# Retention and a rational feed-forward layer on one core: the first four units in quarters, and new orders for steps 0 to 31

## The chip, the core and the metric

One core of a Trainium2 chip. Its engines run their own instruction streams in order and wait for each other by semaphores: PE (TensorE, matmuls into PSUM), DVE (VectorE), ACT (ScalarE), POOL (GpSimd), and SP, whose queue issues all DMAs here. The metric is the device time of one execution in microseconds (us).

## The reference

```python
def _attn_ref(q, k, v):                    # (8, 8, 576, 64): batch, heads, tokens, head size
    scores = (1/sqrt(64)) * q @ k.T
    gamma = 1 - 2.0 ** (-5 - arange(8))    # one per head
    rel = pos[:, None] - pos[None, :]
    Dmat = where(rel >= 0, gamma ** rel, 0)
    return (scores * Dmat) @ v

def _moe_ref(x, w_in, w_out, a, b):        # x: 4608 x 512, w_in: 512 x 2048, w_out: 2048 x 512
    h = x @ w_in
    P = a0 + a1*h + a2*h**2 + a3*h**3
    Q = 1 + |b0|*|h| + |b1|*h**2
    return (P / (Q + 1e-6)) @ w_out
```

`x` is the first function's output, heads side by side. Everything is float32, the weights arrive as float64 bits (read as int64).

## The kernel before, in words

**Retention.** The 4608 tokens are 36 units of 128, for all eight heads (four pairs). The decay matrix is split into factors: q is multiplied by powers of gamma that grow along the unit (`scale_q`), v by powers that fall (`scale_v`), so that only a triangular 0/1 mask is left between scores and output (`decay`), and what came ahead of a unit enters by a state `S` that is carried on (`add`) and faded (`fade`, on POOL). A unit of the later kind is done in quarters, two halves of 64 tokens on either side (`visit`): scores and state sums of unit k on 64x64 matmuls in four corners of the array, and beside them the output of the unit before (`put`, `of_inside`, `of_before`). Its state in the middle of a unit is made by DVE (`middle`). Rows of the array that write one bank are kept apart by a no-op on the SP queue that PE signals and then waits for (`follow`, L377).

Units 0 to 3 are done otherwise in this kernel (`whole_scores`, `whole_state`, `whole_decay`, `whole_outputs`, `whole_add`): 128 tokens at a time, with a 128x128 mask `whole_sb` and a PSUM tile `early` for the state sums. For units 0 to 3 the second layout of k is not loaded but made by four transposes on PE (`turn`) into the PSUM tile `unread`, and a copy by ACT (`keep_turned`, called kn in the orders). Unit n's raw inputs are the tiles qk n and kv n.

**Feed-forward.** Four units make a block of 512 tokens, nine blocks. x is split into a high part (`xhi`, ACT) and a low part (`xlo`, DVE). A step is one block b and one slice f of 128 of the 2048 inner columns: `gemm1` makes h (12 matmuls of 512 columns), then come p, u, v (p the polynomial, u = |h|, v the denominator): `ffn_p` (ACT and DVE), `ffn_p2` (DVE), `ffn_va` (v's linear step, on DVE or ACT by the table VA), `ffn_v` (DVE), `ffn_r` (ACT, Ln and Exp into u), `ffn_q`, `ffn_q3` (DVE), `ffn_hi` (ACT) and `ffn_lo` (the low part of g, on DVE or POOL by LO). `gemm2` of a step comes three or four steps later. Steps 0 to 7 are the first half of block 0, 8 to 23 block 1, 24 to 31 the other half of block 0, and from 32 on block by block. In steps 8 to 20 the tile u lies in PSUM (`free_at`).

**Weights.** Each of 32 weight tiles is loaded as bits and put together by ACT (two instructions, `c` and `bits`, or `held`), merged by DVE (`c<-c,bits`), copied as a high part by ACT (`w`) and its low part made by DVE or POOL (table WLO). All this goes on up to step 23 beside the steps.

**Order.** All four compute engines take instructions in the order in which the program issues them (`InOrder`). That order is written out: `BEFORE0` to `BEFORE4` for the stretch ahead of step 0 (the head), one list a unit; FIRST0 to FIRST23, MID (steps 8 to 20), DENSE and DENSE_ALONE (24 to 31) for the steps; REST from step 32 on. `run` (L650) goes through a list; words whose work there is none of are passed over. STARTS says how many weight tiles are begun in a step, LOADS in which order units and weights are loaded, SCALES and SCALES_Q which engine scales v and q of units 0 to 8.

Of the kernel before, what the change touches and what calls it, by code (L numbers as in the profile page):

```python
# [30 lines left out]
NP = 4  # L31

BEFORE0 = "warm_a outputs warm_b scores split3 turn keep_hi scale_v split1 start kn state split0 scale_q decay add fade split2 keep_lo decay1".split()
BEFORE1 = "turn outputs scale_q scores kn warm_b split0 start keep_hi state warm_a split1 decay add scale_v fade decay1 split3 split2 keep_lo".split()
BEFORE2 = "turn scores scale_v kn split3 split0 outputs warm_a state warm_b keep_hi decay split2 start decay1 scale_q split1 add keep_lo fade".split()
BEFORE3 = "split0 split1 warm_a turn outputs kn scores keep_hi split3 decay split2 state decay1 start keep_lo add scale_q scale_v fade warm_b".split()
BEFORE4 = "split3 outputs state keep_hi scores split0 start keep_lo decay scale_q split1 add scale_v fade split2".split()
FIRST0 = "scale_v split3 gemm1 split2 ffn_hi visit ffn_r scale_q split0 ffn_q decay ffn_p start keep_hi ffn_p2 keep_lo ffn_va ffn_v decay1 gemm2 ffn_lo add split1 ffn_q3 fade".split()
FIRST1 = "visit gemm1 keep_hi decay ffn_p split3 ffn_p2 scale_v ffn_r ffn_va decay1 add split2 fade ffn_q ffn_hi start split1 scale_q keep_lo ffn_v split0 ffn_q3 gemm2 ffn_lo".split()
FIRST2 = "gemm1 visit ffn_hi split1 decay scale_q ffn_p gemm2 split3 split2 keep_hi ffn_lo decay1 add ffn_va scale_v ffn_r ffn_v keep_lo fade start ffn_p2 split0 ffn_q ffn_q3".split()  # L40
# [6 lines left out]
FIRST22 = "visit scale_q split1 gemm1 split0 decay scale_v ffn_p split3 keep_hi decay1 ffn_hi ffn_p2 gemm2 ffn_r ffn_q add keep_lo fade start ffn_lo ffn_q3 split2 ffn_va ffn_v".split()
FIRST23 = "split0 gemm1 ffn_p split3 visit decay ffn_va ffn_v gemm2 ffn_hi scale_q ffn_p2 keep_hi keep_lo split2 decay1 ffn_r add ffn_lo fade ffn_q scale_v split1 ffn_q3 start".split()
MID = "start gemm1 split1 ffn_p ffn_hi ffn_r ffn_p2 gemm2 ffn_va ffn_lo split2 ffn_q ffn_v ffn_q3 split3 split0".split()
DENSE = "scale_q gemm1 visit decay ffn_p split0 ffn_hi split1 ffn_va ffn_r gemm2 ffn_lo keep_hi ffn_v ffn_p2 split2 split3 scale_v ffn_q ffn_q3 decay1 add keep_lo fade".split()  # L50
DENSE_ALONE = "gemm1 ffn_r ffn_p visit decay decay1 ffn_p2 ffn_q keep_hi split2 ffn_va add scale_v ffn_hi split3 ffn_v fade scale_q gemm2 split0 ffn_lo keep_lo ffn_q3 split1".split()
# [6 lines left out]
STARTS_BEFORE = "0 0 2 2 2".split()  # L58
LOADS = "unit | weight unit unit weight weight | weight unit weight weight unit weight | weight".split()
STARTS = "0 2 2 1 3 1 0 1 0 0 1 1 1 1 1 2 1 0 2 2 1 1 1 1".split()  # L60
# [28 lines left out]
def retention_ffn(ctx: ExitStack, tc: tile.TileContext, qkv, w_in, w_out, consts, masks, out):  # L89
# [49 lines left out]
    firsts = op.tile([P, 2, DM], F32, tag="o0", name="whole_sb")[:, 0, 0 : 2 * P]  # L139
    whole_sb, unit_sb = firsts[:, 0:P], firsts[:, P:]  # L140
# [6 lines left out]
    def warm(n, by=None):  # L147
        by = gq_sb[:, 0] if by is None else by
# [86 lines left out]
    def place_of(a, k):  # L235
        by_acc = k is not None and k <= NP and k != 2
# [3 lines left out]
    def places(a, k):  # L240


        apart = a is None or k is not None and k <= NP
# [59 lines left out]
    early = ps_h.tile([P, 2, NPAIR, D], F32, tag="h", name="early")  # L303

    def whole_scores(n):


        q, kt = (raws[n][0][:, i] for i in range(2))
        ps = sums[n] = place_of(None, n)
        for g in range(NPAIR):  # L310
            for j in range(2):
                r = slice(j * D, j * D + D)
                pe.matmul(ps[:, j, g * P : (g + 1) * P], kt[r, g], q[r, g], start=True, stop=True, skip_group_check=True)

# [6 lines left out]

    def whole_state(n):
        kn, v = (raws[n][1][:, i] for i in range(2))
        for g in range(NPAIR):
            for j in range(2):
                o = early[j * D : (j + 1) * D, n % 2, g, :]
                pe.matmul(o, kn[:, 2 * g + j, :], v[:, 2 * g + j, :], start=True, stop=True, skip_group_check=True)

    def whole_ret(n, j):
        return raws[n][0][:, 1] if j == 0 else raws[n][1][:, 0].rearrange("p (g x) d -> p g (x d)", g=NPAIR)  # L330

    def whole_decay(n, j):
        m = whole_sb.unsqueeze(1).broadcast_to([P, NPAIR, P])
        dve.tensor_tensor(whole_ret(n, j), sums[n][:, j].rearrange("p (g i) -> p g i", g=NPAIR), m, ALU.mult)

    def whole_outputs(n):
        q, v, o = raws[n][0][:, 0], raws[n][1][:, 1], sums_of(n)
        for j in range(2):
            ret = whole_ret(n, j)
            for c in range(2):  # L340
                for e in range(2):
                    pe.matmul(o[e * D : (e + 1) * D, j, c, :], v[:, 4 * c + 2 * e + j, :], ret[:, 2 * c + e, :], start=c == 0, stop=True, skip_group_check=True)
        if n % 9:
            for c in range(2):
                for j in range(2):
                    for e in range(2):
                        r = slice(j * D, j * D + D)
                        pe.matmul(o[e * D : (e + 1) * D, j, c, :], state[n][r, 2 * c + e, :], q[r, 2 * c + e, :], start=False, stop=True, skip_group_check=True)

# [333 lines left out]
    def load_more(n):  # L683


        for what in loading:
            if what == "|":
                return
# [91 lines left out]
```

## Time and profile before

| what | us |
|---|---|
| runs (3) | 873.03, 874.12, 875.38 |
| profiled execution | 873.48 |
| its span | 871.7 |
| PE busy | 851.0 (98%) |
| DVE busy | 774.6 (89%) |
| ACT busy | 664.8 (76%) |
| POOL busy | 131.5 (15%) |
| chain that ended last | PE 81%, DVE 11%, ACT 4% |

The span is that of the program's instructions; the execution's own time lies 1.8 us above it. Busy shares are means over stages that differ: in the first stretch PE works in pieces of less than a microsecond and waits between them, from step 32 on it runs without a break.

### The profile page before, as it was taken

To read this page: it belongs to the slowest core of one execution; us is meant where nothing else is said; L and a number is where in the kernel's file an instruction comes from. 1 tells how busy PE (TensorE), PEld (TensorE's weight loads), DVE (VectorE), ACT (ScalarE), POOL (GpSimd) and SP (SyncE) were. 2 spreads that over 40 slices of the span, in tenths; PEclk is the share of its full clock that TensorE was granted. 3 is DMA by queue.
4 is the path that set the end of the run, shared out by engine and by line. 5 is a ranking of instruction groups with operands and counts; after the bars stand their busy time and mean duration, and the time that the engine had idled before them with its cause. 6 is when DMAs were issued, how large, how long until landed. Compare 5 with 4: busy or idle time off the path is not lost.

```text
span 871.7 us, 18740 instructions
## 1 busy us (share of the span) xinstructions
PE 851.0 (98%) x7574; PEld 727.6 (83%) x7574; DVE 774.6 (89%) x1222; ACT 664.8 (76%) x1239; POOL 131.5 (15%) x107
## 2 busy tenths in 40 slices
PE   8899999999999999999999999999999999999996
PEld 7657787778888888888888888888888888888885
DVE  4999999999899888898889988898898899888994
ACT  3898999988767778777877787778777787667773
POOL 2532323621001110111111110000111111000000
PEclk9999999999999999999999999999999999999999
DMA  9895000033121112111211121111211121001001
GB/s 343 310 355 221 1 2 0 2 104 112 36 92 50 49 50 98 49 50 50 97 50 50 49 98 50 49 50 57 70 39 41 42 97 50 1 2 48 1 1 48
DMA packets 20806, 64.55 MB, mean 74 GB/s; under 512 B 2544, under 2 KB 2672, under 8 KB 20720
## 3 DMA queue, kind: packets, MB, share of 16 engines
q1 hardware_dynamic: 20720, 63.36, 20.8%
q8 instruction: 59, 0.97, 0.4%
q14 instruction: 27, 0.22, 0.1%
HBM read 53.91 MB, written 9.44 MB: 73 GB/s over the span
## 4 chain that ended last, share of the span: by engine, by line
PE 81%; DVE 11%; ACT 4%; issue 2%; DMA 1%; POOL 0%; SPq 0%; ACTq 0%; DVEq 0%; POOLq 0%
PE acc L85 37%; PE h L85 36%; DVE p L85 5%; PE ps L85 4%; DVE v L85 3%; PE y L85 2%; DVE c L85 1%; PE psNone L85 1%; ACT free_at L85 1%; ACT g L85 1%; DMA qk<-in_qkv 1%; DVE qk L85 0%; ACT bits L85 0%; ACT c L85 0%; ACT u L85 0%
## 5 line engine op out<-in xcount | busy, mean ns | idle before, releaser
L85 PE MATMUL h<-xhi,w 128*128 128x512 f32 x1152 | 367.8, 381 | 3.9 <-DVE p L85 3.2
L85 PE MATMUL acc<-w,g 128*128 128x512 f32 x1584 | 367.8, 381 | 3.4 <-ACT o L85 1.6
L85 PEld LDWEIGHTS acc<-w,g 128*128 128x128 f32 x1584 | 296.2, 189 | 49.4 <-ACT o L85 2.0
L85 PEld LDWEIGHTS h<-xhi,w 128*128 128x128 f32 x1152 | 217.7, 189 | 38.0 <-DVE p L85 3.1
L85 ACT ACTIVATE p<-h,const_sb 128x512 f32<-128x512 f32 x144 | 111.5, 774 | 164.1 <-PE h L85 157.5
L85 PE MATMUL h<-xlo,w 128*128 128x512 f32 x576 | 218.4, 379 | 0.1
L85 DVE TENSOR_TENSOR p<-p,h 128x512 f32<-128x512 f32 x144 | 98.5, 684 | 41.0 <-ACT u L85 38.6
L85 PEld LDWEIGHTS h<-xlo,w 128*128 128x128 f32 x576 | 108.9, 189 | 16.7 <-issue 1.1
L85 DVE SCALAR_TENSOR_TENSOR p<-p,const_sb,h 128x512 f32<-128x512 f32 x144 | 107.3, 745 | 4.0
L85 ACT ACTIVATE v<-u,absb 128x512 f32<-128x512 f32 x129 | 103.3, 801 | 0.3 <-DVE p L85 0.2
L85 DVE SCALAR_TENSOR_TENSOR p<-v,p 128x512 f32<-128x512 f32 x140 | 99.0, 707 | 3.3
L85 DVE TENSOR_TENSOR v<-v,u 128x512 f32<-128x512 f32 x131 | 101.4, 774 | 0.2 <-ACT v L85 0.2
L85 DVE SCALAR_TENSOR_TENSOR p<-p,const_sb,u 128x512 f32<-128x512 f32 x131 | 99.3, 758 | 1.2 <-ACT u L85 1.2
L85 POOL TENSOR_TENSOR S<-S,const_sb 128x256 f32<-128x256 f32 x32 | 27.1, 848 | 454.9 <-DVE S L85 454.9
L85 DVE SCALAR_TENSOR_TENSOR v<-v,u 128x512 f32<-128x512 f32 x131 | 89.4, 683 | 0.0
L85 ACT ACTIVATE u<-u 128x512 f32<-128x512 f32 x131 | 82.6, 630 | 4.1
L85 ACT ACTIVATE g<-p 128x512 fp32r<-128x512 f32 x132 | 82.7, 627 | 3.4 <-DVE p L85 3.1
L85 ACT ACTIVATE u<-v 128x512 f32<-128x512 f32 x131 | 82.0, 626 | 3.1 <-DVE v L85 3.1
L85 DVE TENSOR_TENSOR g<-p,g 128x512 fp32r<-128x512 f32 x115 | 78.6, 684 | 2.6 <-ACT g L85 2.6
L85 ACT ACTIVATE u<-h 128x512 f32<-128x512 f32 x131 | 76.7, 586 | 2.5 <-DVE v L85 2.4
L85 ACT ACTIVATE kv<-kv,const_sb 128x64 f32<-128x64 f32 x232 | 58.2, 334 | 4.6 <-DMA kv<-in_qkv 4.6
L85 POOL TENSOR_TENSOR qk<-qk,const_sb 128x512 f32<-128x512 f32 x31 | 48.7, 1573 | 39.0 <-DMA qk<-in_qkv 39.0
(93 smaller groups left out, 714.9 us busy)
## 6 DMA issues: line engine op xcount, KB each, us to landing
qk<-in_qkv SPq DMA_DIRECT2D x36, 512.0 KB, 4.1
kv<-in_qkv SPq DMA_DIRECT2D x32, 512.0 KB, 5.9
bits<-in_w_in SPq DMA_DIRECT2D x16, 512.0 KB, 8.8
bits<-in_w_out SPq DMA_DIRECT2D x16, 512.0 KB, 7.4
out<-o SPq DMA_DIRECT2D x28, 256.0 KB, 4.0
out<-o SPq DMA_DIRECT2D x16, 128.0 KB, 2.1
kv<-in_qkv SPq DMA_DIRECT2D x4, 256.0 KB, 6.7
const_sb<-in_consts SPq DMA_DIRECT2D x1, 265.0 KB, 2.9
```

Of the source, the lines that this page charges most:

```text
L85: return lambda *a, **k: self.tc.keep_in_program_order(method(*a, **k))
```

## The change

The four units of the head go through the same functions as later units: `visit(None, n)` for scores and state sums, `decay`, `add`, `fade`, then `put`. The five `whole_` functions, the tile `early` and the 128x128 mask are gone; `turn` and `keep_turned` stay. In place of five lists, the table LOADS and two counts there is one list HEAD with a word for each piece of work and each load, with the unit's number behind it (W is the load of a weight tile, begin starts putting one together, merge and halve carry it on). All lists for steps 0 to 31 but REST and END, and STARTS, SCALES, SCALES_Q, VA, LO and WLO are new.

```diff
-NP = 4
-
-BEFORE0 = "warm_a outputs warm_b scores split3 turn keep_hi scale_v split1 start kn state split0 scale_q decay add ...
...
+HEADED = 4
+
+HEAD = (
+    "U0 M scale_q0 turn0 U1 kn0 scale_v0 visit0 scale_q1 turn1 U2 kn1 turn2 decay0 scale_v1 add0 fade0 visit1"
+    " scale_q2 put0 kn2 decay1 W U3 W add1 W scale_q3 U4 scale_v2 W scale_v3 turn3 hi0 visit2 begin lo0 kn3"
+    " begin fade1 merge0 put1 U5 decay2 hi1 begin add2 merge1 visit3 scale_q4 put2 fade2 halve0 decay3 W add3"
+    " lo1 scale_v4 fade3 hi2 W lo2 begin put3 hi3 scale_v5 merge2 W lo3 visit4 merge3 halve1 halve2 decay4"
+    " begin W add4 fade4 scale_q5 W halve3 begin"
+).split()
...
-SCALES = "scalar pool pool vector pool vector pool scalar pool".split()
-SCALES_Q = "vector vector vector pool pool vector vector pool pool".split()
-VA = "act act act act vector act act vector act vector vector vector vector vector vector act act vector vector vector vector act act act".split()
-LO = "vector pool pool pool pool pool pool pool pool pool pool pool pool vector vector pool pool pool pool pool pool pool vector pool".split()
+SCALES = "pool vector pool pool pool pool pool vector vector".split()
+SCALES_Q = "pool vector vector vector vector vector vector vector pool".split()
+VA = "act act act act vector act act vector act act vector vector vector act vector act act vector act vector act act vector act".split()
+LO = "pool vector vector vector pool pool pool pool pool pool pool pool pool pool pool pool pool pool pool pool pool pool pool pool".split()
...
-    warm(int(WARM[0]), zeros)
+    warm(WARM, zeros)
...
+    def advance(i):
+        for _ in range(2):
+            next(going[i][0], 0)
+            going[i][1] += 1
+
+    def put_alone(n):
+        put(n)
+        done_with(n)
...
+    for word in HEAD:
+        if word in alone:
+            alone[word]()
         else:
...
+            does[word.rstrip("0123456789")](int(word.lstrip("abcdefghijklmnopqrstuvwxyzU_")))
```

How the instructions stand: first PE in the head, from unit 0's scores or transposes on; psNone_n is the PSUM tile of unit n's scores. Before:

```order
L85 MATMUL psNone_0_133<-qk0_112 128x128 x8
L85 MATMUL unread_101<-whole_sb_97,qk0_112 128x128 x4
L85 MATMUL early_110<-kv0_114 64x64 x8
L85 MATMUL unread_101<-whole_sb_97,qk1_117 128x128 x4
L85 MATMUL psNone_0_133<-qk0_112,kv0_114 64x128 x4
L85 MATMUL psNone_0_133<-kv0_114 64x128 x4
L85 MATMUL psNone_1_190<-qk1_117 128x128 x8
L85 MATMUL early_110<-kv1_119 64x64 x8
```

And in the changed kernel:

```order
L86 MATMUL unread_101<-unit_sb_97,qk0_114 128x128 x4
L86 MATMUL psNone_0_131<-qk0_114 64x64 x16
L86 MATMUL psNone_0_131<-kv0_116 64x64 x16
L86 MATMUL unread_101<-unit_sb_97,qk1_125 128x128 x4
L86 MATMUL unread_101<-unit_sb_97,qk2_169 128x128 x4
L86 MATMUL psNone_1_184<-qk1_125 64x64 x16
L86 MATMUL psNone_1_184<-kv1_127 64x64 x16
L86 MATMUL psNone_0_131<-qk0_114,kv0_116 64x64 x24
```

The transposes come ahead of the scores, unit 2's ahead of unit 1's scores, and unit 0's output behind them. On DVE the same stretch ends with block 0's last `xlo` (xlo0). Before, from unit 2's first decay:

```order
L85 TENSOR_TENSOR qk2_177<-psNone_2_222,whole_sb_97 128x512
L85 TENSOR_TENSOR kv2_179<-psNone_2_222,whole_sb_97 128x512
L85 TENSOR_TENSOR S3_283<-S2_212,early_110 128x256
L85 TENSOR_TENSOR xlo0_201<-psNone_1_190,xhi0_200 128x4x128
L85 SCALAR_TENSOR_TENSOR c0_0_275<-c0_0_275,bits0_0_175 128x512
L85 SCALAR_TENSOR_TENSOR c0_1_278<-c0_1_278,bits0_1_185 128x512
L85 TENSOR_TENSOR qk3_181<-psNone_3_312,whole_sb_97 128x512
L85 TENSOR_TENSOR kv3_183<-psNone_3_312,whole_sb_97 128x512
L85 TENSOR_TENSOR xlo0_201<-psNone_2_222,xhi0_200 128x4x128
L85 TENSOR_TENSOR S4_339<-S3_283,early_110 128x256
L85 TENSOR_TENSOR w0_0_344<-c0_0_275,w0_0_344 128x512
L85 TENSOR_TENSOR xlo0_201<-psNone_3_312,xhi0_200 128x4x128
```

In the changed kernel, from the same decay:

```order
L86 TENSOR_TENSOR qk2_169<-psNone_2_274,mask_sb_96 128x512
L86 TENSOR_TENSOR kv2_171<-S2_254,psNone_2_274 128x256
L86 TENSOR_TENSOR S3_360<-kv2_171,psNone_2_274 128x256
L86 SCALAR_TENSOR_TENSOR c0_1_312<-c0_1_312,bits0_1_252 128x512
L86 TENSOR_TENSOR qk4_259<-qk4_259,const_sb_95 128x512
L86 TENSOR_TENSOR qk3_248<-psNone_3_363,mask_sb_96 128x512
L86 TENSOR_TENSOR kv3_250<-S3_360,psNone_3_363 128x256
L86 TENSOR_TENSOR S4_438<-kv3_250,psNone_3_363 128x256
L86 TENSOR_TENSOR xlo0_272<-psNone_1_184,xhi0_271 128x4x128
L86 TENSOR_TENSOR xlo0_272<-psNone_2_274,xhi0_271 128x4x128
L86 SCALAR_TENSOR_TENSOR c0_2_357<-c0_2_357,bits0_2_256 128x512
L86 TENSOR_TENSOR xlo0_272<-psNone_3_363,xhi0_271 128x4x128
```

A decay is one instruction in place of two, the state two of half that size in place of one, and the first weight's low part has left DVE. ACT at step 13 (block 1, slice 5), before:

```order
L85 ACTIVATE p1_5_1309<-h1_5_1294,const_sb_95 128x512
L85 ACTIVATE free_at_1045<-h1_5_1294 128x512
L85 ACTIVATE g1_3_1313<-p1_3_1203 128x512
L85 ACTIVATE free_at_1045<-v1_4_1258 128x512
L85 ACTIVATE free_at_1045<-free_at_1045 128x512
L85 ACTIVATE w0_10_1336<-c0_10_1241 128x512
```

And in the changed kernel:

```order
L86 ACTIVATE p1_5_1426<-h1_5_1409,const_sb_95 128x512
L86 ACTIVATE free_at_1164<-h1_5_1409 128x512
L86 ACTIVATE g1_3_1430<-p1_3_1321 128x512
L86 ACTIVATE free_at_1164<-v1_4_1372 128x512
L86 ACTIVATE free_at_1164<-free_at_1164 128x512
L86 ACTIVATE v1_5_1425<-free_at_1164,absb_98 128x512
L86 ACTIVATE w0_10_1453<-c0_10_1369 128x512
```

v's linear step has come to ACT, behind Ln and Exp of the step before (the two that read v1_4 and then free_at). On the SP queue the load of unit 4's q and k has, beside the wait for an earlier DMA, one for PE in the changed kernel (the put of unit 0), and none before.

## Rows read from the trace of the kernel before

**Rows 1.** The page: shares of the chain that ended last.
```profile
PE 81%; DVE 11%; ACT 4%; issue 2%; DMA 1%; POOL 0%; SPq 0%; ACTq 0%; DVEq 0%; POOLq 0%
```

**Rows 2.** PE's timeline (start us, us, instruction, idle before and releaser).
```profile
8.68 1.12 PE L85 MATMUL unread<-whole_sb,qk 128*128 128x128 f32 x4
...
16.08 0.66 PE L85 MATMUL unread<-whole_sb,qk 128*128 128x128 f32 x4
...
26.96 0.64 PE L85 MATMUL psNone<-qk 64*64 64x64 f32 x32
27.43 0.63 PE L85 MATMUL psNone<-kv 64*64 64x64 f32 x16
...
28.58 0.48 PE L85 MATMUL h<-xlo,w 128*128 128x512 f32 x1
...
31.15 0.46 PE L85 MATMUL ps<-qk,kv 64*64 64x64 f32 x16
...
31.67 0.23 PE L85 MATMUL y<-qk 64*64 64x64 f32 x2
...
32.82 0.41 PE L85 MATMUL ps<-qk,kv 64*64 64x64 f32 x16
...
42.26 0.27 PE L85 MATMUL y<-qk 64*64 64x64 f32 x2 [2.05 <-DVE qk L85]
```

**Rows 3.** DVE's timeline in the head.
```profile
8.88 0.69 DVE L85 TENSOR_TENSOR qk<-qk,const_sb 128x512 f32<-128x512 f32 x1 [2.27 <-DMA qk<-in_qkv]
...
16.27 0.42 DVE L85 TENSOR_TENSOR S<-S,early 128x256 f32<-128x256 f32 x1
16.61 0.68 DVE L85 TENSOR_TENSOR kv<-psNone,whole_sb 128x512 f32<-128x512 f32 x1
17.21 0.68 DVE L85 TENSOR_TENSOR xlo<-psNone,xhi 128x512 fp32r<-128x512 f32 x1
17.81 1.36 DVE L85 TENSOR_TENSOR kv<-kv,const_sb 128x512 f32<-128x512 f32 x1
...
21.72 2.47 DVE L85 SCALAR_TENSOR_TENSOR c<-c,bits 128x512 int32<-128x512 int32 x2
...
27.83 0.69 DVE L85 TENSOR_TENSOR xlo<-psNone,xhi 128x512 fp32r<-128x512 f32 x1 [0.91 <-ACT xhi L85]
```

**Rows 4.** POOL's timeline in the head.
```profile
9.63 1.04 POOL L85 TENSOR_TENSOR kv<-kv,const_sb 128x512 f32<-128x512 f32 x1 [9.19 <-DMA kv<-in_qkv]
...
17.34 1.28 POOL L85 TENSOR_TENSOR qk<-qk,const_sb 128x512 f32<-128x512 f32 x1
```

**Rows 5.** ACT's timeline in the head.
```profile
6.62 2.02 ACT L85 ACTIVATE kv<-kv,const_sb 128x64 f32<-128x64 f32 x8 [4.60 <-DMA kv<-in_qkv]
9.83 0.60 ACT L85 ACTIVATE kv<-unread 128x512 f32<-128x512 f32 x1 [1.20 <-PE unread L85]
```

**Rows 6.** Busy time by stretch: steps 0 to 7, steps 8 to 21.
```profile
core 0: us, PE busy (x) PEld busy (x) DVE busy (x) ACT busy (x) POOL busy (x), PEclk, DMA share, GB/s
33.70:85.10 51.40, 48.99 (x470) 33.37 (x471) 48.58 (x79) 43.89 (x79) 16.23 (x13) 1.00 0.85 316
83.50:162.60 79.10, 74.29 (x340) 63.26 (x339) 77.88 (x119) 74.60 (x121) 27.56 (x21) 1.00 0.00 1
```

**Rows 7.** Groups by form, whole span: v's linear step on DVE and on ACT.
```profile
L85 DVE TENSOR_SCALAR v<-free_at,absb 128x512 f32<-128x512 f32 x10 | 8.1, 806 | 0.2
...
L85 ACT ACTIVATE v<-free_at,absb 128x512 f32<-128x512 f32 x3 | 2.3, 773 | 0.1
```

**Rows 8.** Waits from 83.5 to 162.6 (us in total, times, longest).
```profile
PE h L85 <- DVE p L85: 3.2, 4, 1.3
...
ACT free_at L85 <- DVE v L85: 2.8, 5, 1.0
...
DVE p L85 <- ACT v L85: 0.3, 1, 0.3
```

**Rows 9.** DMA issues (engine, times, size, median us to landing).
```profile
qk<-in_qkv SPq DMA_DIRECT2D x36, 512.0 KB, 4.1
```

More of the change, by code (lines that the diff above doesn't have):

```diff
@@ L30 @@
 NF = DFF // P
-NP = 4
[L33 to L40, printed above, removed]
@@ L47 @@
[L47 to L50, printed above, removed]
@@ L52 @@
+MID = "split1 gemm1 start ffn_p ffn_hi ffn_p2 ffn_r gemm2 ffn_lo split0 ffn_va split2 ffn_q ffn_v ffn_q3 split3".split()
+DENSE = "scale_v gemm1 visit decay decay1 split0 split1 scale_q ffn_p ffn_va ffn_v ffn_hi ffn_lo split2 ffn_r ffn_q keep_hi add ffn_p2 ffn_q3 keep_lo split3 fade gemm2".split()
+DENSE_ALONE = "split3 ffn_r visit gemm1 ffn_p split2 ffn_hi decay split1 split0 scale_q ffn_lo ffn_p2 keep_hi keep_lo decay1 gemm2 ffn_va add ffn_q ffn_q3 fade ffn_v scale_v".split()
 REST = (
@@ L56 @@
 END = "ffn_r ffn_hi gemm2 ffn_lo ffn_q ffn_q3".split()
-STARTS_BEFORE = "0 0 2 2 2".split()
-LOADS = "unit | weight unit unit weight weight | weight unit weight weight unit weight | weight".split()
-STARTS = "0 2 2 1 3 1 0 1 0 0 1 1 1 1 1 2 1 0 2 2 1 1 1 1".split()
+STARTS = "1 3 0 2 2 1 0 1 0 0 0 2 1 1 1 2 1 1 2 1 2 1 0 1".split()
 PLAIN = "0 1 2 3".split()
@@ L235, in place_of @@
     def place_of(a, k):
-        by_acc = k is not None and k <= NP and k != 2
+        by_acc = k is not None and k <= HEADED and k != 2
         pool_, tag = (ps_acc, "acc") if by_acc else (ps_at, "at")
@@ L240, in places @@
     def places(a, k):
-        apart = a is None or k is not None and k <= NP
+        apart = a is None or k is not None and k <= HEADED
         ps = place_of(a, k)
@@ L301, in of_before @@
         return made
[L303 to L313, printed above, removed]
     def turn(n):
@@ L320, in keep_turned @@
         act.activation(raws[n][1][:, 0], unread.rearrange("p (h d) -> p h d", h=H), AF.Copy)
[L322 to L348, printed above, removed]
-    def whole_add(n):
-        S = state[n + 1] = sp.tile([P, NPAIR, D], F32, tag="S", name=f"S{n + 1}")
-        if n % 9 == 0:
-            dve.tensor_copy(S, early[:, n % 2])
-        else:
-            dve.tensor_tensor(S, state[n], early[:, n % 2], ALU.add)
     def emit(*rows_of):
@@ L654, in run @@
                 todo[name][0](*todo[name][1:])
-    def before(n):
-        def outputs():
-            if n == 1:
-                nc.sync.dma_start(mask_sb, masks[:, 2 * P :])
-            whole_outputs(n - 1)
-            done_with(n - 1)
-            load_more(n)
-        todo = {"start": (split_start, int(STARTS_BEFORE[n]))}
-        todo |= {f.__name__: (f, n + 1) for f in (scale_q, scale_v)}
-        if n < NP:
-            todo |= {"scores": (whole_scores, n), "state": (whole_state, n), "add": (whole_add, n), "fade": (fade, n)}
-            todo |= {"decay": (whole_decay, n, 0), "decay1": (whole_decay, n, 1)}
-            todo |= {"turn": (turn, n), "kn": (keep_turned, n)}
-            todo["warm_a"] = warm, int(WARM[n + 1])
-        else:
-            todo |= {"scores": (visit, None, n), "decay": (decay, n), "add": (add, n), "fade": (fade, n)}
-        if n >= 1:
-            todo |= {f.__name__: (f, n - 1) for f in (keep_hi, keep_lo)}
-            todo["outputs"] = (outputs,)
-            if n < NP:
-                todo["warm_b"] = warm, int(WARM[n + 5])
-        run((BEFORE0, BEFORE1, BEFORE2, BEFORE3, BEFORE4)[n], todo)
@@ L680, in retention_ffn @@
-    units = iter(range(1, 6))
-    loading = iter(LOADS)
[L683 to L688, printed above, removed]
-            load_weights(1) if what == "weight" else load_unit(next(units))
-    nc.sync.dma_start(const_sb, consts)
-    load_unit(0)
-    nc.sync.dma_start(firsts, masks[:, 0 : 2 * P])
-    load_more(0)
-    scale_q(0)
-    scale_v(0)
-    for n in range(NP + 1):
-        before(n)
+    def advance(i):
+        for _ in range(2):
+            next(going[i][0], 0)
+            going[i][1] += 1
@@ new lines, in put_alone, with load_masks @@
+    def put_alone(n):
+        put(n)
+        done_with(n)
+    def load_masks():
+        nc.sync.dma_start(unit_sb, masks[:, 0:P])
+        nc.sync.dma_start(mask_sb, masks[:, P:])
+    does = {
+        "U": load_unit, "scale_q": scale_q, "scale_v": scale_v, "turn": turn, "kn": keep_turned,
+        "visit": lambda n: visit(None, n), "decay": decay, "add": add, "fade": fade, "put": put_alone,
+        "hi": keep_hi, "lo": keep_lo, "merge": advance, "halve": advance,
+    }
+    alone = {"M": load_masks, "W": lambda: load_weights(1), "begin": lambda: split_start(1)}
```

34 lines of the change are left out of this document (19 added, 15 removed).

## The prediction

> **What bounds the kernel now.** I read the chain that ended last first: PE holds 81% of it and DVE 11% [rows 1]. So over the whole span the matmuls set the time, and what another engine costs shows only where PE waits for it. The orders from step 32 on are unchanged, so a gain or loss made up to step 31 is carried to the end as it is. Then I read PE's timeline of the head and the steps behind it, row by row, for idle time in brackets and for how long one kind of row takes [rows 2]; DVE, POOL and ACT of the same stretch [rows 3 to 5]; the busy time of all engines in two stretches [rows 6]; and who waited for whom in the second [rows 8].
>
> What is to be seen there: step 0's first matmul on `xlo` starts at 28.58 [rows 2], right after DVE's last `xlo` of block 0, which starts at 27.83 and takes 0.69 [rows 3]. Step 0 is therefore set by DVE. At 42.26 PE has been idle for 2.05 us, again for DVE [rows 2]. From the p of step 0 to that of step 8 (33.70 to 85.10, 51.40 us) PE is busy for 48.99 and DVE for 48.58; from 83.50 to 162.60 (79.10 us, steps 8 to 21) DVE is busy for 77.88, ACT for 74.60, PE for 74.29 [rows 6]. In that second stretch DVE is the bound with ACT close behind, and PE's idle time is what can be won, its waits for DVE's p among it (3.2 us in four [rows 8]).
>
> **The head, step by step.** On DVE the head before step 0's p loses eight decays of 128x512 and gains four of that size; q scalings go from four to five, v scalings from two to one, the weight's low part leaves for POOL. Instead of 24 instructions of 128x512 there are 19, and instead of 7 of 128x256 there are 11: the quarters need the state in the middle of each unit. At 0.60 us from start to start (16.61 to 17.21) and 0.34 (16.27 to 16.61) [rows 3], that is -5 x 0.60 + 4 x 0.34 = -1.6 us of work. The rest of the head's gain is idle time, for which I follow the new order.
>
> PE is at first at what its rows show as the lower of its two clock levels (1.2 and 2.4 GHz): four transposes take 1.12 at 8.68 and 0.66 at 16.08 [rows 2]. Unit 0's v has landed by 6.62 [rows 5]; the unit matrix is the next, 64 KB long, which I put at 6.8 (estimate). Turn 0 runs to 7.9, ACT's copy takes 0.60 [rows 5], to 8.5. POOL scales q of unit 0 meanwhile: 1.04 for such an instruction [rows 4]. Scores in quarters take 0.47 at the upper level (26.96 to 27.43 for unit 4 [rows 2]), so 0.94 here; scores and state of unit 0 end at 9.8. Unit 1's q and k land at 8.9 as before (8.88 [rows 3]). Turn 1 ends at 10.9, its copy at 11.5, turn 2 at 12.6, scores 1 at 13.6.
>
> From there DVE has 18 instructions up to the last `xlo`: eight of 0.60, six of 0.34, three merges of weight words at 1.2 (two took 2.47 beside POOL, 21.72 [rows 3]) and the last `xlo` of 0.69. That is 4.8 + 2.0 + 3.6 + 0.7 = 11.1, so 24.7, and 0.5 for the two waits for ACT's `xhi` and weight words: 25.2. Before, that `xlo` ended at 27.83 + 0.69 = 28.5. **First term: -3.3 us.** PE keeps up if its clock is at the upper level by then: state 1 0.47, four puts at 0.85 (0.52 from 31.15 to 31.67, and 0.3 for the part at 32.82 [rows 2]), turn 3 0.66 and two visits of 0.94 make 6.4, and it waits for DVE. The bounds: merges without POOL beside them take 0.60, and no waits: 22.9, -5.6. With the lower level up to step 0, PE needs 12.8 from 13.6, then `xhi` and `xlo` 1.3: 27.7, -0.8.
>
> A wait is added on the SP queue: the put of unit 0 leaves a no-op there, and the load of unit 4's q and k stands behind it, with unit 4's v, a weight and unit 5 behind that. Put 0 ends at about 15; a q-and-k load takes 4.1 from issue to landing (median [rows 9]), so it lands at 19.2. DVE wants it for its scaling after 6.7 of the 11.1 us and the waits, at 20.3. I take nothing; if the put is late by the lower clock, a microsecond, inside the bounds above.
>
> The Trainium skill, "SBUF — State Buffer", section "SBUF: two separate sides", says that a VectorE instruction with two SBUF inputs and a GpSimd one that reads SBUF exclude each other for a whole instruction. The trace agrees: a v scaling on DVE took 1.36 at 17.81 beside POOL's 1.28 from 17.34 [rows 3, 4], where the like at 8.88 took 0.69. The rule speaks against the change, for POOL takes five of the first six v scalings. Five of the 18 DVE instructions have two SBUF inputs; held once each for a full 0.67 they cost 3.4, where I took 3 x 0.6 = 1.8 for the merges. By the rule's worst the sum below would be 1.6 smaller.
>
> **Steps 0 to 7.** DVE gets one q and one v scaling more (unit 7): 48.58 + 1.4 = 50.0 of 51.4 [rows 6]. ACT loses unit 7's eight small scalings, about 2.0 [rows 5]. The stretch cannot shrink by more than 1.4; of the 2.05 us at 42.26 a part can go since unit 5's v scaling has left DVE. I take -0.4, near the lower side, for DVE is then 98% busy. Bounds -1.4 and +1.
>
> **Steps 8 to 21.** Four of v's linear steps move from DVE (0.806) to ACT (0.773 [rows 7]) at steps 9, 13, 18 and 20, and two low parts from DVE (0.60) to POOL. DVE: 77.88 - 3.2 - 1.2 = 73.5. ACT: 74.60 + 3.1 = 77.7 [rows 6]. What is late next is ACT: the stretch of 79.1 cannot fall below 77.7. I take -1.0 of these 1.4. The rest of MID's new order hardly moves an instruction within one engine, nor does the low part cost PE anything as long as POOL, busy for 27.56 of 79.10 [rows 6], ends it within a step. Steps 22 to 31: one v scaling more on DVE and one low part less; nothing.
>
> **Sum:** -3.3 - 0.4 - 1.0 = -4.7 us. The profiled execution took 873.48, so 868.8; the median of the runs shown is 874.12, 0.64 above, so 869.4.
>
> **Rivals.**
> *The head's gain stays small (same time).* PE does less work in the head and waits more, so the clock may come up later than the 16.08 by which it had doubled [rows 2]. Then the head gives 0.8, and steps 0 to 7 nothing since DVE has more there: -0.8 to -2 us with the third term, 872 to 873. For it: the head's rows at the lower level; against it: PE is without a longer gap from turn 2 on in my walk.
> *ACT becomes the bound of steps 8 to 21 (slower).* Where DVE does v's linear step, it needs only u. Where ACT does, the step stands behind exp of the step before, which waits for DVE's v, and DVE's next waits for it: a loop through two engines. Waits of this kind are there already: ACT's u on DVE's v 2.8 us in five, DVE's p on ACT's v 0.3 [rows 8]. Each step that loses 0.26 us by it undoes the other two terms (14 x 0.26 = 3.7). With 0.45 a step the stretch grows by 6.3, and the time is 874.1 - 3.7 + 6.3 = 876.7. For it: ACT would be at 98% of today's stretch. Against it: ACT is now held up by a DVE that is 98% busy, and that one gets 4.4 us of room.
> *DVE alone sets steps 8 to 21 (more than forecast).* Then its 4.4 us all come off, with the head's 3.3 and 1.4 of steps 0 to 7: -9.1, 865.0. Against it stands ACT's 77.7; PE's own floor, 74.29, would allow it.
>
> **How the numbers follow.** About 0.3%, 2.6 us, is what a measurement of this kernel can tell from no change. The forecast, -2.6 to -7, gets 0.58; more than that 0.08; the small gain 0.20, all within 2.6 us; ACT as the bound 0.14, slower by over 2.6 us. So faster 0.66, same 0.20, slower 0.14. The range: below, the third rival's 865.0; above it has to take in the small gain's 873 and the start of ACT's case, where the other terms are just undone and a little more: 875.0.
>
> **What would show it.** Right: step 0's first matmul on `xlo` near 25.3; the p of step 8 on DVE near 81.4 and that of step 22 about 4.7 earlier than now, with ACT busy for 97% or more in between and DVE for under 95%; transposes of units 1 and 2 still at 1.1 us each. Wrong: matmuls of step 0 at the lower clock level, or that step at 27 or later (first term); DVE idle for unit 4's q (the SP queue); ACT idle more than 2 us for DVE's v in steps 8 to 21 (the second rival); PE's wait of 2.05 us at unit 6 still there (second term).

## The result: slower, 882.1 us

| what | before | after |
|---|---|---|
| median of the runs (us) | 873.58 (4 runs, 872.74 to 875.38) | 882.08 (4 runs, 880.70 to 883.87) |
| span of the profiled execution (us) | 871.7 | 880.9 |
| mean granted clock | 0.998 | 0.987 |
| PE, DVE, ACT, POOL busy (us) | 851.0, 774.6, 664.8, 131.5 | 852.1, 766.7, 663.4, 133.6 |

The ratio is 1.011, 95% interval 1.009 to 1.013. Forecast were 869.4 us and a range up to 875.0: the sign was wrong and the range missed. DVE is busy for 8 us less and PE for as long as before, and yet the time grows by 8.5 us.

Where it grows is read from the first `h<-xhi,w` row of each step in PE's timeline (start, us):

| step | 0 | 3 | 8 | 10 | 22 | 27 | 32 | PE's last row ends |
|---|---|---|---|---|---|---|---|---|
| before | 28.00 | 47.49 | 80.36 | 88.13 | 156.33 | 192.59 | 222.93 | 864.93 |
| after | 30.89 | 55.87 | 88.74 | 97.70 | 166.06 | 201.38 | 231.72 | 873.72 |
| difference | 2.9 | 8.4 | 8.4 | 9.6 | 9.7 | 8.8 | 8.8 | 8.8 |

So 8.4 of 8.8 us are lost by step 3, 2.9 of them in the head. The rows of the kernel before for steps 0 and 3:

```profile
28.00 0.48 PE L85 MATMUL h<-xhi,w 128*128 128x512 f32 x1
...
47.49 0.89 PE L85 MATMUL h<-xhi,w 128*128 128x512 f32 x1
```

PE's timeline of the changed kernel in that stretch (columns as in [rows 2]):

```profile
14.46 0.34 PE L86 MATMUL psNone<-qk 64*64 64x64 f32 x7
16.52 0.62 PE L86 MATMUL psNone<-qk 64*64 64x64 f32 x25 [1.72 <-issue]
...
18.68 0.29 PE L86 MATMUL psNone<-qk 64*64 64x64 f32 x6
22.54 1.01 PE L86 MATMUL psNone<-qk 64*64 64x64 f32 x26 [3.57 <-issue]
...
26.91 0.58 PE L86 MATMUL psNone<-qk,kv 64*64 64x64 f32 x9 [0.22 <-issue]
...
30.89 0.79 PE L86 MATMUL h<-xhi,w 128*128 128x512 f32 x1
31.47 0.63 PE L86 MATMUL h<-xlo,w 128*128 128x512 f32 x1
...
46.92 0.27 PE L86 MATMUL y<-qk 64*64 64x64 f32 x2 [2.25 <-DVE qk L86]
...
49.33 0.48 PE L86 MATMUL ps<-qk,kv 64*64 64x64 f32 x3 [1.03 <-issue]
...
55.87 0.89 PE L86 MATMUL h<-xhi,w 128*128 128x512 f32 x1
```

The reader is to see where the idle time stands: in the middle of one piece of work. Unit 2's scores are 32 rows that need nothing but the two inputs already read, and PE stops after 7 of them for 1.72 us; in unit 3's it stops after 6 for 3.57. The releaser is "issue", nothing that the profile shows. [rows 2] had no such row. DVE, which the forecast made the bound of the head, now waits for PE:

```profile
17.64 0.69 DVE L86 TENSOR_TENSOR qk<-psNone,mask_sb 128x512 f32<-128x512 f32 x1 [1.58 <-PE psNone L86]
...
24.44 0.69 DVE L86 TENSOR_TENSOR qk<-psNone,mask_sb 128x512 f32<-128x512 f32 x1 [3.63 <-PE psNone L86]
```

Next, how many instructions PE had done at each stop: the two counts in brackets in a window that begins at 0 and ends within the break (us; then us busy and, in brackets, instructions of PE, PEld, DVE, ACT and POOL).

```profile
0.00:16.40 16.40, 10.50 (x221) 9.04 (x221) 7.05 (x13) 5.30 (x8) 6.43 (x10) 1.00 0.88 319
0.00:22.40 22.40, 12.85 (x348) 11.12 (x349) 10.11 (x18) 8.79 (x14) 8.66 (x12) 0.98 0.92 345
0.00:26.80 26.80, 16.91 (x476) 14.79 (x476) 12.15 (x22) 9.04 (x15) 10.42 (x15) 0.90 0.87 329
```

442, 697 and 952: the same distance each time. With the 7, 8 and 9 instructions of PE's sequencer that these windows leave out (waits for semaphores, nearly all) the stops lie at 449, 705 and 961, 256 apart. The trace has a DMA queue named "instruction" whose packets in this stretch hold 16,384 bytes, one for each 256 of PE's instructions. So I set up the theory that PE runs out of code: it enters one block, that calls for the block after the next end, and the packet must come through the loads of data (DMA share 0.87 to 0.92 above). Times from the trace's DMA and PE records, of the changed kernel:

```text
PE enters the block   packet of the next    data packets before it begins next block entered
10.50                 14.11 to 15.00        503                           16.52 (break 1.72)
16.52                 20.16 to 21.10        437                           22.54 (break 3.57)
22.54                 24.61 to 25.54        245                           26.91 (break 0.22)
43.22                 46.98 to 47.94        393                           49.33 (break 1.03)
198.30                199.05 to 200.07      0                             210.17 (none)
```

With data under way a block takes 4.4 to 6.1 us from entry to use; without, the packet ends 1.8 us after the entry. (The third column counts the data packets under way between the entry and the start of the code packet.) At 0.47 us for 64 instructions (32 matmuls and their 32 weight loads, unit 4's scores in [rows 2]) quarters want a block every 1.9 us. Up to step 0 PE's instructions grow from 652 to 1164 (x326 and x582 in the windows up to 27.9 and 30.8). The clock follows:

```profile
14.00:21.60 7.60, 3.16 (x138) 2.58 (x139) 5.06 (x8) 5.08 (x9) 3.36 (x4) 1.00 1.03 416
21.60:35.30 13.70, 12.35 (x244) 10.78 (x244) 7.41 (x11) 6.36 (x12) 8.29 (x8) 0.50 0.85 312
35.30:48.90 13.60, 10.05 (x264) 8.41 (x263) 11.32 (x19) 12.34 (x21) 4.46 (x4) 1.00 0.88 319
48.90:55.80 6.90, 6.47 (x10) 2.76 (x10) 6.90 (x13) 3.43 (x6) 3.52 (x3) 0.51 0.98 372
```

PE works at half clock (1.2 GHz) from 21.6 to 35.3, in which step 0 falls, and from 48.9 to 55.8, after waits of 2.25 and 1.03; in the kernel before the granted clock stays at 1.00 from 14.05 on, until the last 4 us:

```profile
21.60:35.30 13.70, 11.79 (x266) 9.68 (x263) 11.96 (x20) 12.17 (x22) 9.04 (x8) 1.00 0.70 258
35.30:47.50 12.20, 10.15 (x156) 6.73 (x154) 12.16 (x22) 10.63 (x19) 5.28 (x4) 1.00 0.98 375
```

The Trainium skill, "Runtime: NRT & Kernel Launch", section "Instruction fetch mechanics", says that code comes in 16 KiB blocks of 256 instructions by a DMA queue of the sequencer's own, and that crossing a block's end is "mostly hidden". The trace agrees on the blocks; hidden it is not here, with 6.5 us of breaks.

### The profile page after: what moved, and what is told of

Same layout as the page of the kernel before. It is cut to its first block, busy times and chain, and to the rows that moved or that the text cites. A ratio compares the mean times of both kernels' runs of the same rounds, so it can differ in the third digit from the quotient of the medians.

```text
span 880.9 us, 19247 instructions
## 1 busy us (share of the span) xinstructions
PE 852.1 (97%) x7830; PEld 728.1 (83%) x7830; DVE 766.7 (87%) x1219; ACT 663.4 (75%) x1226; POOL 133.6 (15%) x109
## 3 DMA queue, kind: packets, MB, share of 16 engines
HBM read 53.85 MB, written 9.44 MB: 72 GB/s over the span
## 4 chain that ended last, share of the span: by engine, by line
PE 83%; ACT 7%; DVE 6%; issue 2%; DMA 1%; SPq 0%; ACTq 0%; DVEq 0%
PE acc L86 38%; PE h L86 37%; PE ps L86 4%; DVE p L86 3%; PE y L86 2%; ACT free_at L86 2%; ACT bits L86 1%; DVE v L86 1%; PE psNone L86 1%; ACT c L86 1%; ACT p L86 1%; ACT w L86 1%; ACT g L86 1%; DMA qk<-in_qkv 1%; DMA kv<-in_qkv 1%
## 5 line engine op out<-in xcount | busy, mean ns | idle before, releaser
L86 POOL TENSOR_TENSOR S<-S,const_sb 128x256 f32<-128x256 f32 x32 | 29.9, 935 | 467.8 <-DVE S L86 446.7
L86 DVE TENSOR_TENSOR v<-v,u 128x512 f32<-128x512 f32 x131 | 97.9, 747 | 0.0
L86 DVE TENSOR_TENSOR g<-p,g 128x512 fp32r<-128x512 f32 x112 | 76.6, 684 | 2.6 <-ACT g L86 2.6
L86 ACT ACTIVATE kv<-kv,const_sb 128x64 f32<-128x64 f32 x216 | 54.2, 334 | 0.0
L86 POOL TENSOR_TENSOR qk<-qk,const_sb 128x512 f32<-128x512 f32 x29 | 46.6, 1607 | 43.5 <-DMA qk<-in_qkv 43.5
```

The costliest lines, as they stand in the source:

```text
L86: return lambda *a, **k: self.tc.keep_in_program_order(method(*a, **k))
```

## Experiments

**1. Head and orders apart.** Two kernels, each with half of the change.

```diff
 orders_alone: the kernel before, with
+FIRST0 ... FIRST23, MID, DENSE, DENSE_ALONE, STARTS, VA, LO, and SCALES, SCALES_Q, WLO from unit 6 and the fourth weight tile on, of the changed kernel
 head_alone: the changed kernel, with these of the kernel before
```

Expected: 

> The head of the kernel before (units 0 to 3 whole, its five lists and LOADS) with the changed kernel's lists and tables for steps 0 to 31. Theory: the loss is made in the head alone, where PE comes to the end of a block of its code (256 instructions) before the next block has landed, and then works on at the lower clock; the new orders are worth 0.8 us from step 10 on. So: PE's rows up to step 0 as before (step 0's first matmul on xlo at 28 to 29), no break in the middle of a unit's scores, granted clock 1.00 from 14 us on, and 871 to 874 us. Rival A (the new lists and tables of steps 0 to 31 make the loss: step 2 to 3 grew by 3.9 us): 877 to 880 us, with PE's wait of 3.5 us for DVE's y at about 35 there too.

> The changed kernel's head with the lists and tables of before for steps 0 to 31. Theory: the breaks of 1.7 and 3.6 us in the scores of units 2 and 3 are there, PE is at the lower clock from about 21 us, step 0 starts at about 31, and the time is 880 to 885 us. Rival A (the new lists and tables make the loss): 871 to 876 us, since step 0 then starts 2.9 us late and nothing more is lost.

Measured: orders_alone 875.31 us, ratio to before 1.0034 (1.0018 to 1.0051); head_alone 878.43, 1.0068 (1.0044 to 1.0093). In head_alone the breaks are 1.80, 2.51, 1.31 and 1.52 us at 16.49, 22.79, 27.99 and 47.40, step 0 starts at 30.31 with the granted clock back at 1.00, and step 3 at 53.85 (before 47.49). Both theories missed: the head makes about two thirds of the loss, the lists and tables about one third. The lists and tables pay at the same place. In orders_alone step 3 starts at 48.54 although step 0 starts at 25.32; a break stands there that the kernel before lacks, and the granted clock is at 0.5 from 40.35 to 47.18:

```profile
39.78 0.27 PE L85 MATMUL y<-qk 64*64 64x64 f32 x2 [2.27 <-DVE qk L85]
...
42.73 0.47 PE L85 MATMUL ps<-qk,kv 64*64 64x64 f32 x2 [0.98 <-issue]
```

**2. A shift of the code by 32 instructions.**

```diff
-WARM = 11
+WARM = 3
```

Expected: 

> The changed kernel with 3 matmuls on zeros at its start instead of 11, 32 instructions of PE's fewer ahead of everything. Theory (end of a block of code): the breaks stay at the same count of PE's instructions (449, 705, 961), so 16 matmul rows later in the work: in unit 2's scores after about 23 of the 32 rows instead of 7; the breaks are shorter by the time that these rows take, 0.2 to 0.5 us each, and the time is 879 to 882 us. Rival B (a wait for another engine or for PSUM): the break stays after 7 rows of unit 2's scores and 6 of unit 3's.

Measured: 882.03 us, 1.0108 (1.0091 to 1.0126). The break at 697 comes 16 rows later in the work, after 22 rows of unit 3's scores instead of 6, at the same count; the next again at 952 (x476 and x476). Work has moved, the count has not: no wait for another engine does that. The first break is gone, though the theory had kept it; the others are longer in sum (4.10 and 1.87, where they were 3.57 and 0.22), so the size was a miss.

```profile
19.26 0.52 PE L86 MATMUL psNone<-qk 64*64 64x64 f32 x22
23.88 0.58 PE L86 MATMUL psNone<-qk 64*64 64x64 f32 x10 [4.10 <-issue]
```

```profile
0.00:23.80 23.80, 13.75 (x348) 11.42 (x349) 9.80 (x18) 8.64 (x14) 9.34 (x13) 0.98 0.89 310
```

**3. Fewer loads ahead of the code.**

```diff
+        if step < 0 and len(issued) >= 3:      # few1: >= 1 and issued[-1]
+            follow(ins, issued[-3])
+        issued.append(ins)
```

Expected: 

> The changed kernel, but each load of a unit's part or of a weight ahead of step 0 waits on the SP queue until the third load before it has landed, so that few bytes are ahead of a block of code. Theory: code packets take 4.4 to 6 us to come because they stand behind the loads of data; with three loads under way a block comes in about 2 us, the breaks of 1.7, 3.6, 0.2 and 1.0 us shrink to under 3 us in sum, the clock stays up for longer, and the time falls to 873 to 879 us. Rival B (the breaks are a wait for a semaphore that the trace does not name: a no-op that keeps writers of one bank apart, or PSUM that is not free): the breaks stay as long and at the same rows, and the time is 882 or, by later data, more.

> As the kernel in which each load ahead of step 0 waits for the third before it (latency of a block of code there 3.3 to 3.5 us from PE's entry into the block before to the packet's end, against 4.1 to 4.7 in the changed kernel), but each waits for the one before it, so that at most one load of 0.25 to 0.5 MB is under way. Theory (code stands behind bytes of data): 1.5 to 2.5 us from entry to the packet's end for the blocks at 193 to 961. Rival C (the time of a block of code does not hang on the data, and is that of the fetch itself): 3.3 us or more again. The kernel's time is no evidence here, since the loads themselves come later: about 890 us.

Measured: few3 885.98 us, few1 931.82 (one run). In few3 the packets end 3.3 to 3.5 us after the entry, where it was 4.1 to 4.6 in three of four blocks (3.0 in the other); in few1 the packets called for by the blocks at 193, 449 and 705 end 2.3, 1.3 and 2.9 us after it (the last over the 2.5 that I gave). So the time of a block does hang on the data under way. The fourth packet came early: at 56.42 to 57.34, while PE stood 12 instructions short of the block at 961 until 64.05. The call can thus run some instructions ahead of PE's rows, and "entry" is only its latest time. In few3 no break is left ahead of step 0, but that is no gain: the time was a miss, by my edit: the no-ops that keep rows of one bank apart stand on the SP queue behind the loads that now wait, and PE waits for them.

```profile
17.18 0.46 PE L86 MATMUL psNone<-qk,kv 64*64 64x64 f32 x16 [2.10 <-SPq L335]
...
24.35 0.46 PE L86 MATMUL psNone<-qk,kv 64*64 64x64 f32 x16 [2.92 <-SPq L335]
```

**4. The first block called for earlier.**

```diff
     warm(WARM, zeros)
+    for _ in range(37):
+        pe.matmul(unread[0:D, 0:D], zeros[0:D, 0:D], zeros[0:D, 0:D], start=True, stop=True)
```

Expected: 

> The changed kernel with 37 more matmuls of 64x64x64 on zeros ahead of unit 0's transposes, while PE waits for the unit matrix anyway (3.5 to 7.2 us). They are 148 instructions, so PE enters the block that begins at its instruction 193 at 5 to 6 us instead of 10.5, and each later end of a block comes 148 instructions earlier in the work. Theory (entering a block calls for the one after the next, which comes 4.4 to 6 us later behind data): the block at 449 is there by 11.5, its break goes; the break at 705 now falls into unit 1's or 2's work and is 1 to 2 us; step 0's first matmul on xlo at 28 to 30 instead of 30.9, and 878 to 881.5 us. More instructions of PE's make the kernel faster. Rival B (a wait for another engine or for PSUM in unit 2's and 3's scores): the breaks stay where they are in the work, step 0 at 30.9 or later, 882 or more.

Measured: 880.91 us, 1.0102 (1.0081 to 1.0124). The breaks moved as the count says (705 now falls into unit 2's state sums, 961 into unit 3's), but a row on one corner of the array took 59 ns, where four corners in turn give 15, so the added work lasted until 10.8 and its block was entered at 10.76, not at 5 to 6. Step 0 came at 32.90, its `xlo` at 33.44 (28 to 30 expected), and the breaks were 0.83, 4.68 and 1.15. The time lies in the range that I gave, but not for the reason given: it decides nothing on the price.

**5. The wait for unit 6's q taken away.**

```diff
 SCALES_Q, unit 6, in the changed kernel (q6_pool) and in the kernel before (before_q6)
-vector
+pool
```

Expected: 

> The changed kernel with the scaling of unit 6's q on POOL, which is free, instead of DVE: PE's wait of 2.25 us for it at 46.92 shrinks to under 0.5. Theory: the block of code at 1729 comes no earlier for it (its packet ends near 47.9 and PE goes on at 49.3), so PE now waits 2.5 to 3.3 us for code where it waited 1.03, step 3 starts at 55.4 to 55.9 as before, and the time is 881 to 882.5 us. Rival D (the wait for DVE is what costs the time there, and the clock that falls after it): step 3 starts 2 to 5 us earlier and the time is 877 to 880 us.

> The kernel before with the same scaling on POOL: its wait of 2.05 us at 42.26 goes. Theory: the block at PE's instruction 1217 was there 0 to 0.3 us ahead of need (packet's end 41.62, and PE goes on some 1.4 us after such an end), so a break of 1 to 2 us appears there instead and the gain is under 1 us: the same within 0.3%. Rival D: step 3 starts 1.5 to 2.1 us earlier and the time is 869.5 to 870.5 us.

Measured: q6_pool 882.46 us, 1.0122 (1.0099 to 1.0144). Its wait of 2.25 us has shrunk to 0.56, and the break behind it grew from 1.03 to 3.12; step 3 starts at 55.43, where it was 55.87:

```profile
45.52 0.27 PE L86 MATMUL y<-qk 64*64 64x64 f32 x2 [0.56 <-POOL qk L86]
...
50.02 0.32 PE L86 MATMUL ps<-qk,kv 64*64 64x64 f32 x2 [3.12 <-issue]
...
55.43 0.89 PE L86 MATMUL h<-xhi,w 128*128 128x512 f32 x1
```

before_q6 took 871.77 us, 1.0004 (0.9986 to 1.0022), and shows a break at 41.00 that the kernel before did not have:

```profile
38.93 0.27 PE L85 MATMUL y<-qk 64*64 64x64 f32 x2 [0.94 <-POOL qk L85]
...
41.00 0.27 PE L85 MATMUL ps<-qk,kv 64*64 64x64 f32 x2 [0.68 <-issue]
```

From step 0 to step 3 it takes 19.42 us, the kernel before 19.49. In both kernels an engine made faster gave nothing that can be told, since code comes no sooner. Rival D fell.

**6. Instructions against time.** Into the kernel before, nearly the same PE time once in few and once in many instructions.

```diff
 before_wide, ahead of unit 4's scores
+            for _ in range(4):
+                x = raws[k][0][:, 0].rearrange("p g i -> p (g i)")
+                pe.matmul(inner[k][0][0].rearrange("p g i -> p (g i)"), x[:, 0:P], x[:, 0 : 2 * P], start=True, stop=True)
 before_more, at the same place
+            for _ in range(8):
+                emit(of_scores(k, 0), of_scores(k, 1))
```

Expected: 

> The kernel before with work for nothing on PE just ahead of unit 4's scores: four matmuls 128x128 on 256 columns, written where the scores then overwrite them; 16 instructions, about 3.4 us. It is the control of the next kernel. PE has 0.6 to 1.1 us of waits there that take up a part, and DVE runs on beside it. All theories: no break, step 0 later by 1.5 to 3 us, and 873 to 876 us.

> The kernel before with unit 4's scores computed nine times instead of once (the last one counts): as much time on PE, 3.8 us at 0.47 us each, but in 512 instructions instead of 16. Theory (a block of 256 instructions of PE's takes at least 4.4 to 6 us while data is loaded): the breaks that the kernel before did not have appear, at PE's instructions 705 and 961 and in the middle of the repeated scores; step 0 starts 3 to 6 us later than in the kernel with wide matmuls, and the time is 877 to 883 us. Rival B (the number of instructions is no matter; the changed kernel waited for something else): the same time as with wide matmuls within 1.5 us, and no break.

Measured: before_wide 875.88 us, 1.0034 (1.0016 to 1.0052), no break; before_more 885.20, 1.0134 (1.0111 to 1.0158).

```profile
25.26 2.62 PE L85 MATMUL psNone<-qk 128*128 128x256 f32 x40
...
28.28 0.48 PE L85 MATMUL h<-xhi,w 128*128 128x512 f32 x1
```

```profile
25.72 3.09 PE L85 MATMUL psNone<-qk 64*64 64x64 f32 x198
32.63 1.55 PE L85 MATMUL psNone<-qk 64*64 64x64 f32 x89 [3.82 <-issue]
...
34.63 0.48 PE L85 MATMUL h<-xhi,w 128*128 128x512 f32 x1
```

```profile
0.00:32.50 32.50, 23.72 (x476) 20.48 (x476) 15.38 (x24) 15.71 (x32) 10.64 (x14) 1.00 0.95 363
```

The kernel before, which never stopped for code, now stops at the changed kernel's count of 952 (none at 697, where I expected one too; 0.63, 0.94 and 0.86 us at later ends), and takes 9.3 us more than the control; 2.0 us of that is that its rows are longer (3.09 + 1.55 against 2.62). It was slower than I gave (877 to 883).

**7. The changed head with half as many PE instructions.** Each quarter matmul of the head works on 128 columns, two pairs of heads, instead of 64, with the first pair's weights for both; the second pair's own products are left out.

```diff
+        if k <= HEADED:
+            return [[(bank, t, out_[cut[t], g : g + 2, :], kt[r, g, cut[t]], q[r, g : g + 2, cut[t]]) for t in range(2)] for g in (0, 2)]
         return [[(bank, t, out_[cut[t], g, :], kt[r, g, cut[t]], q[r, g, cut[t]]) for t in range(2)] for g in range(NPAIR)]
 (and in the same way in of_state, of_inside and of_before)
```

Expected: 

> The changed kernel with half the number of matmuls in the head's quarters (units 0 to 3, and unit 4's scores and state): each works on 128 columns of two pairs of heads with the first one's weights, so PE streams as many columns, the other engines do the same work and the loads are the same, but 544 of PE's some 1150 instructions ahead of step 0 are gone. (The computation changes by it: those units' scores, state and output are wrong for every second pair.) It asks what the prediction's first term would be worth if PE did not run out of code. Theory: no break in the scores of units 1 to 3, step 0's first matmul of xlo at 25 to 27 as the prediction walked it, and 869 to 875 us, the upper part if a break remains in steps 0 to 3 as in the kernel with the head of before and the new lists (875.3). Rival E (the head in quarters is slow by its waits for DVE, ACT or loads, and the breaks only fill time that would be lost anyway): step 0 at 29 or later and 878 us or more.

Measured: 874.52 us, 1.0017 (1.0001 to 1.0032). No break in the head (the first, 0.60, at 56.32), and most of the loss is gone: it is 1.7 us slower than the kernel before measured beside it (872.86), where the changed kernel was 8.5 slower. A part of that is the break of 1.03 us ahead of step 3, which the lower count has moved away too. Step 0's first matmul on `xlo` is a little late, at 27.32, and what holds it is now this:

```profile
21.19 0.69 DVE L86 TENSOR_TENSOR qk<-qk,const_sb 128x512 f32<-128x512 f32 x1 [2.00 <-DMA qk<-in_qkv]
```

```profile
23.39 0.45 PE L86 MATMUL psNone<-qk,kv 64*64 64x128 f32 x8 [3.29 <-DVE S L86]
...
27.32 0.63 PE L86 MATMUL h<-xlo,w 128*128 128x512 f32 x1
```

DVE waits for unit 4's q, and the granted clock is at 0.5 from 24.35 to 31.18. DVE's last `xlo` of block 0 ends at 26.5, where the prediction had 25.2:

```profile
25.80 0.69 DVE L86 TENSOR_TENSOR xlo<-psNone,xhi 128x512 fp32r<-128x512 f32 x1 [0.67 <-ACT xhi L86]
```

So with the instructions halved the walk through DVE holds to 1.3 us, in part by chance: the wait of 2.00 us was not in it, and its three merges at 1.2 took 0.68 each.

**8. A kernel meant to beat both.**

```diff
 before_q6, with
+FIRST22, FIRST23, DENSE, DENSE_ALONE of the changed kernel
```

Expected: 

> The kernel before with the scaling of unit 6's q on POOL and the changed kernel's lists for steps 22 to 31 alone (FIRST22, FIRST23, DENSE, DENSE_ALONE): from step 22 to 27 the changed kernel took 35.3 us where the kernel before took 36.3, with no loads in the way. Theory: this gain does not hang on the head, so 0.5 to 1 us less than the kernel before, at the edge of what can be told: 870.5 to 872.5 us where the kernel before takes 872.8. Rival: steps 18 to 22, where the changed kernel lost 0.55, paid for it, and nothing is gained.

Measured: 883.66 us, 1.0119 (1.0099 to 1.0139), a clear miss. The lists without the tables that belong to them make a new wait, which the changed kernel does not have: unit 8's q stands on POOL behind a weight's low part that waits for ACT. Which table would have spared it was not tested.

```profile
164.61 1.27 POOL L85 TENSOR_TENSOR w<-c,w 128x512 fp32r<-128x512 f32 x1 [3.53 <-ACT w L85]
165.83 1.79 POOL L85 TENSOR_TENSOR qk<-qk,const_sb 128x512 f32<-128x512 f32 x1
```

```profile
167.68 1.13 PE L85 MATMUL psNone<-qk 64*64 64x64 f32 x32 [5.12 <-POOL qk L85]
```

## Why the prediction was wrong

**The step that failed: "PE keeps up if its clock is at the upper level by then".** I added PE's work from the times of its rows, 6.4 us from 13.6 on, and had it wait for DVE. In truth PE was ahead of my walk (unit 2's scores began at 14.46), the clock was at the upper level from 4.6 to 21.6 us, and it still needed until 31.47 for `xlo` where I gave 25.3. What I had not counted is instructions. The bound of -0.8 and the rival of a small gain took the clock for PE's only risk, the bound of -5.6 was about DVE; the time of a block of code was in none of them, so the range could not hold it. Experiments 2, 6 and 7 show this cause. All traces together agree with it: ten of the fourteen kernels have breaks of PE that stand inside one piece of work and have no releaser, 26 in all (0.14 us and more); every one lies at the end of a block (PE's instruction 193 + a multiple of 256, within one), and PE goes on 1.2 to 1.6 us after the end of a code packet. For the part that falls to the clock there is no kernel of its own. Of the signs of being wrong that I had named, three came: step 0's matmuls at the lower clock, `xlo` after 27, and the wait at unit 6.

**The base of the term was itself partly chance.** In three further kernels with the old head (orders_alone, before_q6, mix) step 0 starts at 25.32, 25.77 and 25.37, against 28.00 in the execution on which the sum was made, whose clock came up at 14.05 instead of 6.2 to 6.5. Against those, 25.3 for `xlo`, 0.6 later than the step's start, would have been a gain of 0.6 to 1.1 us rather than 3.3. And step 0 of the changed kernel, at 30.89, is 5.1 to 5.6 us later than in them, not 2.9.

**The SP queue, costed at nothing.** I took 4.1 us from issue to landing for unit 4's q and k [rows 9], the median of all 36. From 10 to 31 us it is 9.8 in the kernel before, a row that I could have read, and 6.3 in the changed kernel:

```profile
qk<-in_qkv SPq DMA_DIRECT2D x3, 512.0 KB, 9.8
```

```profile
qk<-in_qkv SPq DMA_DIRECT2D x3, 512.0 KB, 6.3
```

That the load landed at 19.1 in the changed kernel, where I gave 19.2, is luck: it was issued at 12.86, not at 15, and took 6.25. DVE came to it at 19.70. Without the breaks (half_count) it cost DVE 2.00 us. A median over the span does not hold for the stretch in which DMA is full.

**Steps 0 to 7, -0.4.** Wrong: steps 0 to 3 lose 5.5 us (24.98 from step 0 to step 3, before 19.49), by the break of 1.03 us and the two stretches at half clock. In these, step 0's 12 matmuls take 4.95 us to the start of the next piece (30.89 to 35.84), before 3.15 (28.00 to 31.15), and the eight `acc` matmuls ahead of step 3 take 6.13 (49.74 to 55.87), before 3.91 (43.58 to 47.49): 4.0 us together. The wait that I hoped to shrink stayed (2.05, now 2.25), and experiment 5 shows that its end would have given nothing. From step 3 to step 8 both take 32.87.

**Steps 8 to 21, -1.0.** The busy times came out as worked out, the gain did not. From ACT's p of step 8 to that of step 22 in the changed kernel (columns as in [rows 6]):

```profile
91.90:172.60 80.70, 75.28 (x340) 63.78 (x341) 74.10 (x112) 78.61 (x127) 32.20 (x25) 1.00 0.00 1
```

DVE has 74.1 (I gave 73.5) and ACT 78.6 (77.7), 97% of the stretch; and this wait is there, which was 0.3 us in one [rows 8]:

```profile
DVE p L86 <- ACT v L86: 3.2, 5, 0.9
```

So the rival in which ACT becomes the bound was right in kind: from step 10 to step 22 ACT is busy for 67.40 of 68.36 us (before 64.75 of 68.20) and DVE for 62.57 (67.01), and the gain of 1.0 did not come. Its price was 0.2 us there, and not 6.3. Steps 8 to 22 lose 1.4 us (PE takes 77.32, before 75.97), but 1.2 of it between steps 8 and 10, where PE waits for DVE's second p of step 7:

```profile
92.42 0.48 PE L86 MATMUL h<-xhi,w 128*128 128x512 f32 x1 [0.93 <-DVE p L86]
```

That is ahead of the first v step that moved to ACT (step 9), so the loop through ACT does not explain it. In FIRST7 `ffn_p2` now stands behind `ffn_va` and `ffn_v`, before it stood ahead of them; no run tests that alone, but steps 8 to 10 take 8.96 or 8.97 us in all eight kernels with the new list and 7.77 in all six with the old. Most of the 1.4 comes back from step 22 to 27 (35.32, before 36.26). Over steps 8 to 31 the new lists lose 0.4 us. The sign that I had named for this rival, ACT idle for DVE's v, fell from 2.8 to 1.4 us: I had the waiting engine the wrong way round.

## What to carry to other kernels

Count an engine's instructions as well as their time: where PE's pieces take 15 ns a row and DMA is full, a block of 256 instructions that PE had to wait for took 4.0 to 7.2 us in the runs here, and an edit that cuts work into more pieces pays for it even if every piece fits. A break in the middle of one piece of work, with no releaser, at equal distances in the count, is the mark of it; then a wait removed ahead of the block's end gained nothing here. Take durations of transfers from the stretch in question, and be wary of orders without the tables they were made for (experiment 8).

## What the runs showed that I had not expected

- A block of code takes 1.8 us from PE's entry into the block before to the packet's end when no data packet comes between, and 4.5 with 503.
- The clock does not fall after every break: before_more stops for 3.82 us at 28.8 to 32.6 and its granted clock stays at 1.00 until 51.3; the changed kernel falls at 21.6, within its break of 3.57.
- Matmuls on one 64x64 corner of the array take 59 ns a row (early_block, 7.2 to 10.8 us), on four corners in turn 15, both at a granted clock of 1.00.
- The same head starts step 0 anywhere from 25.3 to 28.0 us, with the time at which the clock first comes up.
